# Second feed-forward layer, tokens 512 to 4607: GEMM2 as seven products behind all of GEMM1, w_out factors streamed from DRAM, output transposed

## The chip, the cores and the metric

One Trainium2 chip, one core. The metric is the device time of one execution in microseconds (us). Clock figures are the granted clock of TensorE as a share of full speed.

## The reference, cut to what matters

```python
attn_out = _attn_ref(q, k, v)                     # chunks of 64, 8 heads x 64
x = attn_out.transpose(0, 2, 1, 3).reshape(B * S, H * D)      # 4608 x 512, float32
...
h = x @ w_in          # layer 0: 512 -> 2048
x = (h * np.cos(h)) @ w_out                       # 2048 -> 512
...
h = x @ w_in          # layer 1, other weights
g = h * (1.0 / (1.0 + np.exp(-1.702 * h)))
return (g @ w_out).astype(np.float32)             # 4608 x 512
```

`GEMM1` is `x @ w_in` and `GEMM2` is `g @ w_out`. The change concerns GEMM2 of layer 1.

## The kernel before, in words

Every operand of a matmul is kept as a pair of a high part and a low part (`split`, lines 187 to 189: ScalarE copies the high part, VectorE subtracts it to get the low part), and every product of two pairs takes three matmuls: high by high, high by low, low by high. All large matmuls have a 128x128 stationary tile and 512 moving columns and add up in one PSUM bank.

The 4608 tokens are nine slices `j` of 512, the 2048 hidden columns are 16 tiles `f` of 128. In each layer the first slices run the ordinary way (`plain`): for each `f`, `gemm1` (12 matmuls, line 489), the activation, and two steps later `gemm2` (12 matmuls, line 587). The remaining slices run in pairs of 1024 tokens (`by_1024`, `pair_of_slices`). There GEMM1 of two slices and two hidden tiles is done with seven products instead of eight (the Strassen-Winograd scheme): sums and differences of the blocks of `x` (`right_factor`) and of `w_in` (`left_factors`, kept in DRAM as `wc`) are multiplied by six matmuls per product (`product`, line 837), and the results are added up in PSUM (`pu`, `pc`, `pb`) and on VectorE (`plus`, line 858).

GEMM2 is ordinary everywhere: 12 matmuls per `f` and slice. In a pair of slices, GEMM2 of slice `ja` stands between the products of GEMM1, one hidden pair behind (`run(6)`, `run(10)`, `run(8)` take its matmuls from a list), while the activations of slice `jb` are parked in SBUF (`park`); after the last pair of tiles comes GEMM2 of slice `jb` alone (`split_park`, `gemm2`). In layer 1 the activation is the stationary operand and `w_out` the moving one, so that the output has tokens on partitions and is stored by rows.

In layer 1, slice 0 is ordinary, and slices 1 to 8 are four pairs; I call each pair a stretch. During slice 0 `w_out` of layer 1 is still being converted from 64-bit floats (`split_w`: four VectorE operations, two or three of ScalarE, and one accumulating transfer from POOL's queue per tile), and the seven sums of `x` for the first stretch are made.

The order of the instructions on TensorE is the program's own (`manual_schedule` on PE). The other engines and the DMA queue of SyncE (SP, which issues nearly all transfers, in order) are ordered by a scheduler that places each instruction where it expects it to be ready. Buffers: eight temporaries of 128x512 (`tp`), two PSUM banks each for `pu` and for `pb`/`pc`, four for GEMM2's sums, three pairs for split activations (`gp`), and two buffers each of `xh` and `xl` (8 KB per partition) in `xp`, into which the factors of `w_in` are loaded one hidden pair ahead (`load_factors`).

## Time and profile before

| | |
|---|---|
| median of 3 runs | 1615.75 us (1613.85 to 1616.1) |
| the profiled execution | 1616.11 us, its span 1614.3 us |
| TensorE (PE) matmuls | 1574.7 us busy, 98% of the span |
| TensorE weight loads (PEld) | 1294.2 us, 80% |
| VectorE (DVE) | 989.0 us, 61% |
| ScalarE (ACT) | 885.1 us, 55% |
| POOL | 42.2 us, 3% |
| data moved | 322.14 MB, mean 200 GB/s |
| granted clock, mean | 0.992 |

The span is the time from the first to the last instruction of the profiled execution; its own time is 1.8 us longer. Matmuls are pipelined, so that the busy time of PE is longer than what PE needs: a matmul of 512 columns is shown with 389 ns, and the next one starts before it ends. The time per matmul is better read from the chain of waits, which gives whole runs of matmuls with their count.

### The profile page before, as it was taken

What the parts mean: (1) busy time and instruction counts of PE and PEld (TensorE: products, weight loads), DVE (VectorE), ACT (ScalarE), POOL (GpSimd) and SP (SyncE); (2) the same over time, 40 slices, a digit from 0 to 9 for tenths busy, and PEclk for the clock granted to TensorE, in tenths of its full rate; (3) what the DMA queues carried; (4) which work ended last, traced back from release to release, by engine and by line L of the source; (5) the groups of instructions that cost most, each with busy time, mean ns of one, the idle gap of its engine ahead of it and who ended that gap; (6) DMA issues with size and microseconds to landing.
All of it is one profiled execution on the core that took longest, in us unless ns stands there. A gap on an engine that the chain in (4) does not pass through costs nothing.

```text
span 1614.3 us, 23505 instructions
## 1 busy us (share of the span) xinstructions
PE 1574.7 (98%) x9024; PEld 1294.2 (80%) x9024; DVE 989.0 (61%) x1621; ACT 885.1 (55%) x1545; POOL 42.2 (3%) x53
## 2 busy tenths in 40 slices
PE   5898999999999999999999999999999999999998
PEld 4677888888888888888878888888888888888887
DVE  7796656787877687778665744455444544454442
ACT  6787656777765777567764633343334333433332
POOL 1221000000000000000000100000000000000000
PEclk9899999999999999999999999999999999999999
DMA  9999224468987798858899425440534053404210
GB/s 355 339 302 320 99 76 160 131 209 301 306 318 276 255 311 279 325 195 308 323 325 346 95 70 204 157 156 1 209 151 163 0 208 134 180 0 183 114 69 26
DMA packets 99328, 322.14 MB, mean 200 GB/s; under 512 B 10768, under 2 KB 10768, under 8 KB 84880
## 3 DMA queue, kind: packets, MB, share of 16 engines
q1 hardware_dynamic: 92448, 308.32, 52.9%
q0 software_dynamic: 6768, 12.32, 4.3%
q8 instruction: 71, 1.16, 0.3%
q14 instruction: 41, 0.34, 0.1%
HBM read 247.46 MB, written 60.82 MB: 191 GB/s over the span
## 4 chain that ended last, share of the span: by engine, by line
PE 92%; DMA 2%; issue 2%; ACT 2%; DVE 1%; SPq 0%; POOL 0%; POOLq 0%; DVEq 0%; ACTq 0%
PE y L587 47%; PE pu L837 19%; PE pc L837 9%; PE h L489 9%; PE pb L837 5%; PE x L411 1%; PE pt_ps L385 1%; PE s L304 1%; DMA i<-wt 1%; DMA raw_o<-w_out 1%; DMA wo<-wo 1%; ACT a L352 0%; DVE wt L234 0%; ACT a L340 0%; DVE wt L228 0%
## 5 line engine op out<-in xcount | busy, mean ns | idle before, releaser
L587 PE MATMUL y<-o,gh 128*128 128x512 f32 x1152 | 299.4, 389 | 0.0
L587 PEld LDWEIGHTS y<-o,gh 128*128 128x128 f32 x1152 | 216.3, 188 | 44.8
L837 PE MATMUL pu<-x_t,w_xh 128*128 128x512 f32 x672 | 207.7, 390 | 0.0
L587 PE MATMUL y<-gh,wo 128*128 128x512 f32 x768 | 203.1, 393 | 1.2 <-DMA wo<-wo 1.2
L587 PEld LDWEIGHTS y<-gh,wo 128*128 128x128 f32 x768 | 142.3, 188 | 32.1 <-ACT gh L188 2.5
L587 PE MATMUL y<-o,gl 128*128 128x512 f32 x576 | 158.4, 389 | 0.0
L189 DVE TENSOR_TENSOR gl<-park,gh 128x512 fp32r<-128x512 f32 x112 | 77.2, 689 | 116.6 <-PE y L587 115.6
L837 PEld LDWEIGHTS pu<-x_t,w_xh 128*128 128x128 f32 x672 | 125.6, 188 | 27.8 <-DVE part L858 1.9
L489 PE MATMUL h<-xh,i 128*128 128x512 f32 x384 | 132.3, 407 | 15.1 <-DVE r L528 10.1
L188 ACT ACTIVATE gh<-park 128x512 fp32r<-128x512 f32 x112 | 70.5, 629 | 126.9 <-PE y L587 126.7
L837 PE MATMUL pu<-x_t,w_xl 128*128 128x512 f32 x336 | 130.9, 390 | 0.0
L587 PEld LDWEIGHTS y<-o,gl 128*128 128x128 f32 x576 | 108.2, 188 | 22.4
L813 ACT ACTIVATE r<-part 128x512 f32<-128x512 f32 x96 | 60.3, 628 | 94.2 <-DVE part L858 94.2
L188 ACT ACTIVATE gh<-r 128x512 fp32r<-128x512 f32 x112 | 70.8, 632 | 69.1 <-DVE r L814 51.0
L189 DVE TENSOR_TENSOR gl<-r,gh 128x512 fp32r<-128x512 f32 x112 | 77.4, 691 | 49.6 <-ACT gh L188 47.1
L858 DVE TENSOR_TENSOR part<-pu,part 128x512 f32<-128x512 f32 x112 | 77.1, 689 | 47.3 <-PE pu L837 43.7
L587 PE MATMUL y<-gl,wo 128*128 128x512 f32 x384 | 105.8, 390 | 0.0
L489 PEld LDWEIGHTS h<-xh,i 128*128 128x128 f32 x384 | 75.2, 196 | 33.8 <-DVE r L528 11.7
L587 PE MATMUL y<-gh,o 128*128 128x512 f32 x384 | 101.5, 403 | 0.0
L858 DVE TENSOR_TENSOR part<-pc,part 128x512 f32<-128x512 f32 x56 | 38.6, 690 | 82.6 <-PE pc L837 68.4
L587 PEld LDWEIGHTS y<-gl,wo 128*128 128x128 f32 x384 | 72.1, 188 | 15.8 <-DVE gl L189 0.8
L587 PEld LDWEIGHTS y<-gh,o 128*128 128x128 f32 x384 | 71.8, 192 | 15.3
(122 smaller groups left out, 2776.3 us busy)
## 6 DMA issues: line engine op xcount, KB each, us to landing
w_xh<-wc SPq DMA_DIRECT2D x56, 1024.0 KB, 5.8
w_xl<-wc SPq DMA_DIRECT2D x56, 1024.0 KB, 8.1
wo<-wo SPq DMA_DIRECT2D x96, 512.0 KB, 4.9
qk<-qk SPq DMA_DIRECT2D x36, 512.0 KB, 6.3
raw_i<-w_in SPq DMA_DIRECT2D x32, 512.0 KB, 7.5
raw_o<-w_out SPq DMA_DIRECT2D x32, 512.0 KB, 9.3
wc<-i SPq DMA_DIRECT2D x64, 256.0 KB, 6.1
wc<-s_part SPq DMA_DIRECT2D x64, 256.0 KB, 4.6
```

The source lines that it names most:

```text
L188: nc.scalar.activation(out=hi, in_=src, func=AF.Copy)
L189: nc.vector.tensor_tensor(out=lo, in0=src, in1=hi.bitcast(F32), op=ALU.subtract)
L304: nc.tensor.matmul(out=s[e][o0:o0 + CH, w, h, :], lhsT=t[p0:p0 + CH, 0, h, o0:o0 + CH], rhs=t[p0:p0 + CH, 1, h, o0:o0 + CH],)
L385: nc.tensor.transpose(pt_ps[:, b, :], a[:, e, w, h0:h0 + 2, :].rearrange("p g k -> p (g k)"), ident)
L411: nc.tensor.matmul(out=xs[i][o0:o0 + CH, b, w, c * CH:(c + 1) * CH], lhsT=t[p0:p0 + CH, c, b, e, :], rhs=pt[p0:p0 + CH, e * (HP // 2) + b, ...
L489: nc.tensor.matmul(out=h, lhsT=a[:, w0], rhs=b[:, k, :], start=(k == 0 and i == 0), stop=(k == KD - 1 and i == 2),)
L587: nc.tensor.matmul(out=ys[d0], lhsT=a, rhs=b, start=(f == 0 and i == 0), stop=(f == NF - 1 and i == 2),)
L813: nc.scalar.activation(out=r, in_=h, func=AF.Sigmoid, scale=1.702)
L837: nc.tensor.matmul(out=out, lhsT=x, rhs=y, start=(start and k == 0 and n == 0), stop=(stop and k == 1 and n == 2), skip_group_check=True,)
L858: nc.vector.tensor_tensor(out=t, in0=more, in1=t, op=ALU.add)
```

## The change: what it does

1. GEMM2 of each stretch is made of seven products too. Its blocks are 1024 hidden columns by 512 tokens (`b11`, `b21`, `t1`, `t2` and three sums of these) and quarters of `w_out` (`a11`, `a12`, four sums, `a22`). A product is eight items (one per hidden pair `i`), an item is six matmuls (two output tiles by three), so GEMM2 of a stretch is 56 items. The order of products is 0, 1, 3, 2, 4, 5, 6.
2. All of GEMM1 of a stretch comes first (products of hidden pairs `i` and `i+1` interleaved), with nothing of GEMM2 between. The activations stay in SBUF as `G[i]` (the tiles `o0` to `o15`, where `w_out` stood), already as the differences `t1` and `t2`. Splitting them into high and low parts (`factor`) runs seven items ahead of the item that uses it (`RING`).
3. The seven factors of `w_out` are made during slice 0 (`left_factors2`, `half_factors2`) and stored in DRAM as `wq`, 256 KB at a time. In each stretch 16 chunks of `wc` and 14 chunks of `wq`, 1 MB each, are streamed through the four buffers of `xp` (`stream1`, `streamed`): a chunk is asked for when the one four before it has been used.
4. `w_out` is now the stationary operand in layer 1 too, and the output has its 512 columns on partitions; it is declared 512x4608, stored as blocks of 128x512 (`store_out`), and turned round on the host, outside the measured time.

Cut to its core (`right_factor` and `split` are unchanged):

```diff
-                ps_y.tile([P, N if layer == 0 else DM], F32, tag=f"y{d}", name=f"y{d}")
+                ps_y.tile([P, N], F32, tag=f"y{d}", name=f"y{d}") for d in range(nd)
...
-            if layer == 0:
-                a, b = ((wh[:, d], gh), (wl[:, d], gh), (wh[:, d], gl))[i]
-            else:
-                a, b = ((gh[:, d], wh), (gh[:, d], wl), (gl[:, d], wh))[i]
+            a, b = ((wh[:, d], gh), (wl[:, d], gh), (wh[:, d], gl))[i]
...
+    ORDER2 = (0, 1, 3, 2, 4, 5, 6)
...
+    def left_factors2(i):
...
+        def whole(k):
+            hi, lo = W[1, "o", 2 * i + k]
+            c[k] = tp.tile([P, DM], F32, tag="t", name="w32")
+            nc.vector.tensor_tensor(out=c[k], in0=hi.bitcast(F32), in1=lo.bitcast(F32), op=add)
...
+                nc.vector.tensor_tensor(out=o, in0=p, in1=q, op=op)
...
+            both = ap.tile([P, 2, DM], F32R, tag="a", name="s_part")
+            split(both[:, 0], both[:, 1], c["uw"[k]])
...
+            nc.sync.dma_start(
+                out=wq[m][i // 4][:, i % 4].bitcast(F32),
+                in_=src[:, :, half * H2:(half + 1) * H2].bitcast(F32),
+            )
...
+    def streamed(n, last):
+
+        ST.pop(n)
+        if n + 4 < NS or not last:
+            stream1((n + 4) % NS)
...
+        def factor(n):
...
+            if m < 4:
+                src = (b11, b21, t1, t2)[m]
+            else:
+                src = tp.tile([P, N], F32, tag="t", name="gs")
...
+                nc.vector.tensor_tensor(out=src, in0=a, in1=b, op=op)
+            split(hi, lo, src)
...
+        product(0, 1)
+        product(0, 0)
+        for m in rest:
+            gemm2(*m)
...
+        for m in (2, 3, 5):
+            product(0, m)
...
+        for i in range(NP - 1):
+            for m in (1, 4, 0, 2, 6, 3, 5):
+                product(i if m in (4, 6) else i + 1, m)
+            factor(i)
+        product(NP - 1, 4)
+        item(0)
+        factor(RING)
+        product(NP - 1, 6)
...
+        for n in range(1, len(items)):
+            item(n)
+            factor(n + RING)
+            if n % 7 in (1, 4) and n > 3 and todo:
+                right_factor(1, ja + 2, *todo.pop(0))
...
+    for i in range(NP):
+        at((1, 0, min(2 * i + 2, NF - 1)), half_factors2, i, 0)
```

Up to the third step of slice 0 of layer 1, all five engines have the same instructions in the same order as before. Three places after that:

TensorE, in the second stretch before: GEMM2 of slice `ja` (`y`, two moving parts of `w_out` per stationary tile `gh`) stands between the products `pc`, `pu`.

```order
L837 MATMUL pc_10980<-x_b221_10641,w_xh_10851 128x512
L837 MATMUL pc_10980<-x_b220_10640,w_xl_10853 128x512
L587 MATMUL y3_10858<-o2_8691,gh_10913 128x512 x2
L587 MATMUL y0_10855<-o2_8691,gl_10914 128x512
L587 MATMUL y1_10856<-o2_8691,gl_10914 128x512
```

TensorE at the same kind of place in the change, at the end of GEMM1 of the first stretch (`pu` of the last hidden pair, product 4), and on into GEMM2 (`q`, with the streamed factor `w_q`):

```order
L913 MATMUL pu<-x_t_9500,w_s 128x512
L978 MATMUL q_10411<-gh,w_q 128x512
L978 MATMUL q_10411<-gl,w_q 128x512
...
L913 MATMUL pu<-x_t_9704,w_s 128x512
...
L978 MATMUL q_10411<-gf,w_q 128x512 x3
L978 MATMUL q_10412<-gf,w_q 128x512 x3
```

Product follows product in GEMM1, one product of GEMM1 is left between the first two items, and from there items follow without a break.

VectorE in slice 0 of layer 1, between the activation of step 4 (`r<-h`) and that of step 5, before:

```order
L537 TENSOR_TENSOR r_9043<-h_9026,r_9043 128x512
L217 TENSOR_SCALAR wt_9049<-wt_9049 128x512
L222 TENSOR_SCALAR wt_9049<-wt_9049 128x512
L228 SCALAR_TENSOR_TENSOR wt_9049<-raw_o8_8796,wt_9049 128x512
L544 TENSOR_TENSOR gl_9087<-r_9043,gh_9086 128x512
L234 SCALAR_TENSOR_TENSOR wt_9049<-raw_o8_8796,wt_9049 128x512
L189 TENSOR_TENSOR x_t11_9191<-chain_9192,x_t10_9190 128x512
L189 TENSOR_TENSOR x_t11_9191<-chain_9196,x_t10_9190 128x512
```

and in the change:

```order
L236 SCALAR_TENSOR_TENSOR wt_9034<-raw_o7_8787,wt_9034 128x512
L801 TENSOR_TENSOR w32_9083<-o2_8705 128x512
L801 TENSOR_TENSOR w32_9085<-o3_8760 128x512
L548 TENSOR_TENSOR gl_9140<-r_9073,gh_9139 128x512
L814 TENSOR_TENSOR su_9087<-w32_9083,w32_9085 128x256
...
L814 TENSOR_TENSOR sw_9088<-w32_9085,su_9087 128x256
...
L191 TENSOR_TENSOR s_part_9093<-su_9087,s_part_9093 128x512
L230 SCALAR_TENSOR_TENSOR wt_9102<-raw_o8_8810,wt_9102 128x512
L191 TENSOR_TENSOR s_part_9096<-sw_9088,s_part_9096 128x512
```

Eight operations for the factors of `w_out` (two `w32`, four of 256 columns, two low parts `s_part`) now stand in every second step beside the conversion `wt`.

SP's queue at the beginning of the first stretch in the change: chunks of `w_in` factors (`w_s`) behind the last stores of `w_out` factors (`wq`) and slice 0's output:

```order
L857 DMA w_s_9753<-wc1_1_103 128x2x1024
L822 DMA wq2_1_131<-s_part_9729 128x2x256
L620 DMA out_0<-yo_9801 128x512
...
L620 DMA out_0<-yo_9810 128x512
L822 DMA wq3_1_133<-s_part_9729 128x2x256
L822 DMA wq4_1_135<-s_part_9732 128x2x256
L822 DMA wq5_1_137<-s_part_9732 128x2x256
L857 DMA w_s_9837<-wc1_2_104 128x2x1024
```

The chunk in the last row belongs to the third hidden pair; eight smaller transfers stand in front of it since the chunk before.

## Rows read from the trace of the kernel before

**Rows 1.** The page: its head, part 1, and part 4 by engine.

```profile
span 1614.3 us, 23505 instructions
...
PE 1574.7 (98%) x9024; PEld 1294.2 (80%) x9024; DVE 989.0 (61%) x1621; ACT 885.1 (55%) x1545; POOL 42.2 (3%) x53
...
PE 92%; DMA 2%; issue 2%; ACT 2%; DVE 1%; SPq 0%; POOL 0%; POOLq 0%; DVEq 0%; ACTq 0%
```

**Rows 2.** Stages: stretch, length, busy PE PEld DVE ACT POOL, clock, DMA share, GB/s.

```profile
966.84:1128.60 161.76, 161.76 (x715) 134.00 (x715) 75.51 (x114) 62.46 (x105) 0.00 (x0) 1.00 0.35 130
...
1452.00:1609.00 157.00, 157.00 (x694) 130.10 (x693) 60.55 (x89) 52.89 (x88) 0.00 (x0) 1.00 0.25 94
```

**Rows 3.** Chain of waits, second stretch: start, length, engine, tile, line, matmuls.

```profile
1234.76 43.52 PE y L587 x192
1278.28 1.36 PE pb L837 x6
```

**Rows 4.** Chain of waits, slice 0 of layer 1.

```profile
864.84 2.72 PE h L489 x12
867.56 2.72 PE y L587 x12
870.28 2.72 PE h L489 x12
...
946.44 2.72 PE h L489 x12
949.16 2.72 PE y L587 x12
951.88 1.36 PE pb L837 x6
```

**Rows 5.** VectorE in order of time, slice 0: start, length, line, operation.

```profile
897.05 0.69 DVE L774 TENSOR_TENSOR chain<-x,chain 128x512 f32<-128x512 f32 x1
897.65 0.42 DVE L222 TENSOR_SCALAR wt<-wt 128x512 uint32<-128x512 uint32 x1
897.99 0.68 DVE L544 TENSOR_TENSOR gl<-r,gh 128x512 fp32r<-128x512 f32 x1
898.59 0.68 DVE L228 SCALAR_TENSOR_TENSOR wt<-raw_o,wt 128x512 uint32<-128x512 uint32 x1
899.19 0.68 DVE L774 TENSOR_TENSOR chain<-x,chain 128x512 f32<-128x512 f32 x1
899.79 0.68 DVE L234 SCALAR_TENSOR_TENSOR wt<-raw_o,wt 128x512 uint32<-128x512 uint32 x1
```

**Rows 6.** VectorE operations on 256 columns: shortest, median, longest in ns.

```profile
L670 DVE TENSOR_TENSOR su<-w x8: 424/426/427, 164.2 to 335.8; 128x256 f32<-128x256 f32 x8
```

**Rows 7.** Stages of 40 us in slice 0, columns as in Rows 2.

```profile
880.00:920.00 40.00, 40.00 (x179) 33.12 (x178) 33.59 (x61) 25.39 (x46) 6.95 (x8) 1.00 0.57 150
920.00:960.00 40.00, 40.00 (x178) 33.16 (x177) 17.25 (x28) 16.14 (x28) 2.61 (x3) 1.00 0.25 73
```

**Rows 8.** Transfers of 1 MB in the first stretch, median us to landing.

```profile
w_xh<-wc SPq DMA_DIRECT2D x8, 1024.0 KB, 4.8
w_xl<-wc SPq DMA_DIRECT2D x8, 1024.0 KB, 6.8
```

**Rows 9.** The same for w_xl in the whole span.

```profile
L749 SPq DMA_DIRECT2D w_xl<-wc x56: 320/384/1628, 239.3 to 1531.5; - x56
...
DMA to landing us min/median/max: 4.8/8.1/13.3
```

**Rows 10.** Stores of left factors (s_part) to DRAM, 256 KB each.

```profile
L674 SPq DMA_DIRECT2D wc<-s_part x64: 319/320/1596, 166.0 to 782.5; - x64
...
DMA to landing us min/median/max: 2.0/4.6/6.6
```

**Rows 11.** ScalarE in order of time, slice 0.

```profile
911.61 0.62 ACT L243 ACTIVATE o<-wt 128x512 fp32r<-128x512 f32 x1
912.13 0.66 ACT L214 ACTIVATE wt<-raw_o 128x512 f32<-128x512 f32 x1
912.68 0.63 ACT L254 ACTIVATE o<-o 128x512 fp32r<-128x512 f32 x1
```

**Rows 12.** The end of the span, in order of time.

```profile
1609.73 0.39 PE L587 MATMUL y<-o,gl 128*128 128x512 f32 x1
1610.15 0.69 DVE L611 TENSOR_SCALAR yo<-y 128x512 f32<-128x512 f32 x1 [0.67 <-PE y L587]
```

More of the change, by code (lines that the diff above doesn't have):

```diff
@@ L128, in tile_chunk_attention_two_moe @@
     NU = qk.shape[0]
-    NT, DM = out.shape
+    DM, NT = out.shape
     NF = w1_in.shape[0]
@@ L182, in tile_chunk_attention_two_moe @@
     wo = [dr.tile([P, 2 * DM], F32R, name=f"wo_{f}") for f in range(NF)]
+    wq = [[dr.tile([P, 4, 2, 2 * P], F32R, name=f"wq{m}_{h}") for h in range(2)] for m in range(7)]
     J0 = 3
@@ L242, in p5 @@
             c["hi"], c["lo"] = w[:, :DM], w[:, DM:]
+            if layer == 1 and which == "o":
+                O1[f] = w
             nc.scalar.activation(out=c["hi"], in_=c["t"], func=AF.Copy)
@@ L567, in gemm2_list @@
         wh, wl = W[layer, "o", f]
-        nd = KD if layer == 0 else UB
+        nd = KD
         if f == 0:
             Y[layer, j] = [
-                ps_y.tile([P, N if layer == 0 else DM], F32, tag=f"y{d}", name=f"y{d}")
-                for d in range(nd)
+                ps_y.tile([P, N], F32, tag=f"y{d}", name=f"y{d}") for d in range(nd)
             ]
@@ L607, in flush_y @@
         for d, y in enumerate(ys):
-            o = tp.tile([P, N if layer == 0 else DM], F32, tag="t", name="yo")
+            o = tp.tile([P, N], F32, tag="t", name="yo")
             scale = -2.0 if layer == 0 else 1.0
@@ L616, in flush_y, with store_out @@
             else:
[L617 to L618 removed]
+                store_out(j, d, o)
+    def store_out(j, d, o):
+        nc.sync.dma_start(out=out[d * P:(d + 1) * P, j * N:(j + 1) * N], in_=o)
     steps = [(l, j, f) for l in range(2) for j in range(NB) for f in range(NF)]
@@ new lines, in half_factors2, with stream1 @@
+    def half_factors2(i, k):
+        if k == 0:
+            SF[i] = left_factors2(i)
+        for fn in SF[i][:-1] if k == 0 else SF.pop(i)[-1:]:
+            fn()
+    ST = {}
+    def stream1(n):
+        if n < 2 * NP:
+            t = xp.tile([P, 2, 4, 2 * P], F32R, tag=("xh", "xl")[n % 2], name="w_s")
+            src = wc[1][n // 2][:, :, 4 * (n % 2):4 * (n % 2) + 4, :]
+            nc.sync.dma_start(
+                out=t.bitcast(F32), in_=src.rearrange("t p o c -> p t o c").bitcast(F32)
+            )
+        else:
+            m, h = divmod(n - 2 * NP, 2)
+            t = xp.tile([P, 4, 2, 2 * P], F32R, tag=("xh", "xl")[n % 2], name="w_q")
+            nc.sync.dma_start(out=t.bitcast(F32), in_=wq[ORDER2[m]][h].bitcast(F32))
+        ST[n] = t
@@ L782, in tile_chunk_attention_two_moe @@
     PARK = {}
     def park(layer, i):
-        if layer == 0:
-            t = wp.tile([P, 2, N], F32, tag=f"o{4 + i}", name="park")
-        elif i < 2:
-            t = qkp.tile([P, 2, N], F32, tag="qk", name="park")
-        elif i < 4:
-            t = ap.tile([P, 2, N], F32, tag="a", name="park")
-        elif i < 6:
-            t = wp.tile([P, 2, N], F32, tag=f"i{NF - 6 + i}", name="park")
-        else:
-            return [vp.tile([P, N], F32, tag="v", name="park") for _ in range(2)]
+        t = wp.tile([P, 2, N], F32, tag=f"o{4 + i}", name="park")
@@ L1199, in tile_chunk_attention_two_moe @@
         rest = [(1, 0, NF - 2), (1, 0, NF - 1)]
+        stream1(2)
+        stream1(3)
         for ja in range(1, NB, 2):
-            last = ja + 2 == NB
-            step_extra = {}
-            if not last:
-                step_extra[0] = [(load_x1, (ja + 2,)), (load_x1, (ja + 3,))]
-                for n, (m, k) in enumerate(RIGHT):
-                    step_extra.setdefault(4 + n // 2, []).append((right_factor, (1, ja + 2, m, k)))
-            rest = by_1024(1, ja, rest, {}, step_extra, last)
-        for m in rest:
-            gemm2(*m)
-        flush_y(1, NB - 1)
-_OUTS = [((4608, 512), "float32")]
+            rest = stretch1(ja, rest, ja + 2 == NB)
+_OUTS = [((512, 4608), "float32")]
 def kernel(q, k, v, moe_w_in, moe_w_out, moe2_w_in, moe2_w_out):
```

162 lines of the change are left out of this document (157 added, 5 removed).

## The prediction, made before the change was run

> **What bounds the kernel now.** I read the page first, then the chain of waits, then the stages. In the head of the page PE is 98% busy and the other compute engines 55 to 61%; the chain that ended last lies on PE for 92% of the span [rows 1]. That alone doesn't say whether matmuls or gaps set the pace, so I looked at the stretches that the change touches: in each of them PE is busy all the time at a granted clock of 1.00 [rows 2]. The chain there is an unbroken run of matmuls: 192 of GEMM2 in 43.52 us, that is 226.7 ns each, and 1.36 us for the six of one product of GEMM1, the same rate [rows 3]. Slice 0 before it is just as dense: gemm1 and gemm2 in turn at 2.72 us per 12 [rows 4]. So in layer 1 time is the number of matmuls times 226.7 ns, as long as everything else keeps out of the way. VectorE and ScalarE have room in a stretch (75.5 and 62.5 us busy of 161.8) and so have the DMA engines (share 0.35) [rows 2]. Slice 0 is the fuller place: VectorE is busy 33.59 of 40 us in its first part and 17.25 in the next [rows 7].
>
> **What the change removes.** GEMM2 of a stretch was 2 slices x 16 tiles x 12 = 384 matmuls; it becomes 56 items x 6 = 336. GEMM1 stays at 336. Four stretches save 4 x 48 = 192 matmuls (the program's count of large and small matmuls falls from 7872 to 7680, the same 192). They have the same shape and the same kinds of operands, so I price them at the rate of the chain: **192 x 226.7 ns = 43.5 us** [rows 3]. The removed ones lie on the path that sets the end. Swapping stationary and moving operand in slice 0's gemm2 leaves count and shape as they were: nothing.
> The Trainium skill ("TensorE: Matmul & The Clock Gate", section "Wait — 56ns, not 53.3ns?") gives 215.7 ns for the step from one 512-column matmul to the next at 2.4 GHz. By it the saving would be an estimated 41.4 us and the result 2.1 us higher. The row is of this kernel and this is its full clock too, so the sum keeps 226.7.
>
> **What the change adds, VectorE first.** Its price is not the busy time in the rows. An operation of 512 columns is shown with 0.68 to 0.69 us, but in a dense run the next one starts 0.60 us after it (897.99, 898.59, 899.19, 899.79), and a short one of 0.42 us takes 0.34 of the queue [rows 5]. Sums of 256 columns are shown with 0.42 us [rows 6]; I take 0.34 likewise. ScalarE's step is 0.52 to 0.55 us [rows 11].
>
> *Slice 0.* The factors of `w_out` cost, per hidden pair, four operations of 512 columns and four of 256: 4 x 0.60 + 4 x 0.34 = 3.8 us, eight times, one every two steps (10.9 us of PE, [rows 4]). In the first 40 us, 61 operations show 33.59 us, which is 33.59 - 61 x 0.09 = 28.1 us of queue [rows 7, 5]; four pairs add 15.0, together 43 in 40 us. VectorE falls about 3 us behind and catches up in the next 40 us (17.25 - 28 x 0.09 + 15.0 = 30). What waits for it is gemm1 two steps on, which needs the PSUM bank of `h` that the sigmoid product has read: 10.88 - 2.72 = 8.2 us after gemm1 has ended, less about 1.3 us for ScalarE and that product, so 6.9 us of slack. Hidden, with 4 us to spare. From below nothing can be gained here. From above: with the full 0.69 and 0.42 us per operation, 33.59 + 4 x 4.44 = 51.4 in 40 us, 11.4 behind, less 6.9: 4.5 us. I take 0, since the dense rows are of this very place.
> ScalarE adds two copies per hidden pair, 1.1 us per 10.9: hidden. They reuse the two `s_part` buffers, so they wait for the stores of the pair before, 10.9 us earlier. Those stores land in 4.6 us, 6.6 at most [rows 10]; the new ones have runs of 1 KB instead of 2, and even twice as long, 13.2, would hold ScalarE 2.3 us, less than the slack of 6.9. The 56 stores are 14.7 MB in some 86 us, beside 150 and 73 GB/s [rows 7]: 0.
>
> *GEMM1 alone.* A round (seven products, 42 matmuls, 9.5 us) gives VectorE three additions, four activation products, two differences and one low part: 10 x 0.60 = 6.0 us, 63%. ScalarE has eight operations, 4.3 us. With GEMM2 gone from between, a bank that is read must be free two products later (2.72 us); the reading addition takes 0.69. Cost 0 where at most two others stand before it in the queue. At the beginning of the last three stretches only one product (1.36 us) lies between; the rest of a GEMM2 in VectorE's queue could cost 0 to 0.7 us three times. I take 0.
>
> *GEMM2.* An item lasts 1.36 us. Products 0 to 3 need one low part per item, 0.60 us; products 4 to 6 two operations, 1.2 us, still under 1.36. The 22 operations of `right_factor` for the next stretch stand early in the order, between the end of GEMM1 and the 16th item, where there is room: 22 x 0.60 = 13.2 us beside 16 x 0.6 = 9.6 in some 24 us. The ring gives each split the time of six items, 8.2 us. In a whole stretch VectorE has some 180 operations, 108 us of 152: hidden.
>
> *The stream.* Each stretch reads 30 MB instead of 16, about 1 MB per 5.1 us, 206 GB/s. A chunk is asked for when the one four before is used up. In GEMM1 that leaves eight products until it is needed, 10.9 us; in GEMM2 12 items, 16.3 us. 1 MB lands in 4.8 us, and the second of two asked for together in 6.8 [rows 8]; over the whole span 8.1 at the median and 13.3 at worst [rows 9]. The tight place is the first stretch, where stores and outputs stand before a chunk on SP. Bounds 0 and 13.3 - 10.9 = 2.4 us; the rows of the stretch itself are the nearest, so I take 0.5.
>
> *The end* stays: the last bank's copy of 0.69 us follows the last matmul [rows 12], then a store of the same size.
>
> **The sum.** Against the profiled execution: 1616.1 - 43.5 + 0.5 = 1573.1. That execution is 0.4 us over the median of the runs (1615.75), so the median should be **1573 us**. With the unknown costs at their ends (0 to 4.5, 0 to 2.1, 0 to 2.4) this case runs from 1572 to 1581, and single runs differ by 1 us to either side.
>
> **The rivals.**
> *VectorE at its full price.* If an operation holds the queue for its whole 0.69 us, slice 0 loses 4.5 us and nothing else does: in the late products 2 x 0.69 = 1.38 us per item against 1.36 is covered by the ring. 1573 + 4.5 = 1577.5. Against it: the dense rows step by 0.60 [rows 5].
> The Trainium skill ("VectorE: DVE Perf Modes", section "The TRN2 errata — SBUF-src ops pay a fixed extra latency per instruction") speaks for this rival: it gives 691 ns for a float32 sum of two tensors at 512 columns and says the latency shows between instructions. The busy time in the rows agrees with the 691, the step in the dense run doesn't. 8%.
> *GEMM1 without its filling.* With GEMM2 between the products a late addition cost nothing. Now, if two or three more operations stand before it on VectorE, 4 x 0.60 + 0.69 = 3.1 us against 2.72, each round loses 0.4 us or somewhat more, in 32 rounds some 12: 1585. For it: all readers of PSUM share two in-order queues. Against: 63% load. 10%.
> *The stream becomes the bound (slower than before).* If 1 MB took on average L us from request to landing in the stretches, each of the 32 rounds would wait L - 10.9. From L = 12.3 on this eats the whole 43.5 us; at 12.5 it gives 1624. For it: twice the data, and 13.3 us has been seen once under load [rows 9]. Against: 4.8 to 6.8 in a stretch, at a DMA share of 0.35 that would rise to about 0.6 [rows 2, 8]. 5%.
> *It doesn't save matmuls* is ruled out by the count.
>
> **How the numbers follow.** The forecast has 75%, VectorE's full price 8, GEMM1's gaps 10, the stream 5; 2 are left for stalls that cancel most of the gain. About 0.2% (3.2 us) is what a measurement of this kernel can tell from no change. All but the last two cases lie far below that: faster 0.94, same 0.01, slower 0.05. The range 1570.5 to 1584 holds the forecast with its bounds, the first rival and the mild half of the second.
>
> **What would show it.** Right: in the chain of the stretches, runs of PE without others, 152.3 us each (672 matmuls), VectorE 65 to 80% busy there, DMA share about 0.6, slice 0 still 86 us. Wrong in slice 0: waits of PE for the sigmoid product `r` or `gl`, and VectorE at 9 tenths over two slices of the page. Wrong in GEMM1: waits of `pu` or `pc` for `part`. Wrong in the stream: waits for DMA `w_s` or `w_q`, above all on the third hidden pair of the first stretch. The prediction as a whole is wrong if the matmuls in a stretch no longer follow each other at 226.7 ns.

## The result, and the profile after

The changed kernel takes **1574.51 us** (median of four runs, 1573.32 to 1575.34), the kernel before 1614.92 us (four runs, 1613.85 to 1616.1). The ratio is 0.9751, with a 95% interval of [0.9739, 0.9763]: faster by 40.4 us. The prediction was 1573.0 us with a range from 1570.5 to 1584. The profiled execution of the changed kernel took 1574.87 us, its span is 1573.1 us.

The head of the page and its lists by engine (busy time; the chain that ended last), after:

```profile
span 1573.1 us, 23852 instructions
...
PE 1531.2 (97%) x8832; PEld 1256.3 (80%) x8832; DVE 1169.5 (74%) x1953; ACT 958.3 (61%) x1669; POOL 42.3 (3%) x53
...
PE 85%; DVE 5%; DMA 5%; issue 3%; ACT 2%; SPq 0%; POOL 0%; POOLq 0%; DVEq 0%; ACTq 0%
```

They answer to [rows 1]. PE is as full as before (97% against 98%), and VectorE has risen from 61 to 74%. The chain is new in one way: a part of it now lies on VectorE and on DMA. The stages tell where. In the windows after (PE, PEld, DVE, ACT, POOL busy; granted clock, DMA share, GB/s) the first two rows are slice 0 of layer 1, the next three are the first three of the four stretches:

```profile
880.00:920.00 40.00, 39.77 (x176) 32.58 (x175) 36.28 (x72) 25.02 (x44) 6.00 (x7) 1.00 1.06 318
920.00:960.00 40.00, 39.27 (x172) 31.63 (x171) 39.85 (x78) 24.12 (x42) 3.70 (x5) 1.00 0.91 258
966.84:1119.20 152.36, 151.54 (x669) 125.07 (x668) 113.88 (x181) 78.21 (x133) 0.00 (x0) 1.00 0.73 249
1119.20:1271.50 152.30, 152.30 (x674) 126.02 (x673) 114.25 (x182) 78.92 (x133) 0.00 (x0) 1.00 0.66 232
1271.50:1423.80 152.30, 152.30 (x673) 126.04 (x672) 112.12 (x178) 78.91 (x133) 0.00 (x0) 1.00 0.63 221
```

The stretches are what they should be: 152.30 us for 672 matmuls, VectorE 74 to 75% busy, DMA share 0.63 to 0.73; before they took 161.8 us [rows 2]. PE is busy all the time from the second stretch on; in the first it has gaps of 0.82 us together. Slice 0 is not as it was [rows 7]: the DMA share went from 0.57 to 1.06 and from 0.25 to 0.91, VectorE has next to no idle time left in the second row (0.15 us), and PE has gaps (39.77 and 39.27 of 40). The chain inside the stretches is an unbroken run of matmuls of GEMM2, 74.80 us for 330, 226.7 ns each, as in [rows 3]:

```profile
1037.22 74.80 PE q L978 x330
1189.58 74.80 PE q L978 x330
1341.93 74.80 PE q L978 x330
```

What PE still waits for, from slice 0 to the end (weight load and what released it: us in total, times, longest):

```profile
PEld h L493 <- DVE r L541: 1.4, 3, 0.7
PEld pb L913 <- DMA w_s<-wc: 1.2, 1, 1.2
PEld y L587 <- DVE gl L548: 1.2, 1, 1.2
PEld pu L913 <- DVE part L886: 0.5, 3, 0.2
```

A weight load may wait while PE still has work, so these times are upper bounds of what PE lost; they are the list of places. The first and third rows lie in slice 0 or at its end (`r`, three times; `gl` of its last tile), the second is the chunk of the third hidden pair in the first stretch. The last row is one wait of 0.2 us at the end of GEMM1 in each of the first three stretches; the kernel with 4 stores (below) has the same three and loses nothing, so they cost PE nothing. No stretch after the first has a wait of PE for the stream.

**A better yardstick than the span.** Layer 0 and all that comes ahead of slice 0 is the same work in every kernel here, but it doesn't end at the same moment in each execution. In time order of PE, the first matmul of slice 0 starts before and after at

```profile
864.68 0.39 PE L489 MATMUL h<-xh,w 128*128 128x512 f32 x1
```

```profile
863.82 0.39 PE L493 MATMUL h<-xh,w 128*128 128x512 f32 x1
```

So I count from there to the end of the span: 1614.3 - 864.68 = 749.6 us before, 709.3 after. The predicted 43.5 us would leave 749.6 - 43.5 = **706.1**; the changed kernel loses 3.2 us against that. The experiments below are read by this count, which takes out the early part's variation of some 2 us (4 with the kernel whose stores POOL issues).

Each row of the table below is one execution. Three kernels in it have the same slice 0 and the same stores as the changed kernel, which loses 3.2 us: they lose 3.1 us (GEMM1's products twice), 4.0 us (lead of three chunks) and 752.1 - 43.5 - 706.1 = 2.5 us (192 more matmuls). So rows that differ by 1 us or so can't be told apart.

### The profile page after: what moved, and what is told of

Read it like the earlier page. It is cut to its first block, busy times and chain, and to the rows that moved or that the text cites. A ratio compares the mean times of both kernels' runs of the same rounds, so it can differ in the third digit from the quotient of the medians.

```text
span 1573.1 us, 23852 instructions
## 1 busy us (share of the span) xinstructions
PE 1531.2 (97%) x8832; PEld 1256.3 (80%) x8832; DVE 1169.5 (74%) x1953; ACT 958.3 (61%) x1669; POOL 42.3 (3%) x53
## 4 chain that ended last, share of the span: by engine, by line
PE 85%; DVE 5%; DMA 5%; issue 3%; ACT 2%; SPq 0%; POOL 0%; POOLq 0%; DVEq 0%; ACTq 0%
PE y L587 23%; PE q L978 19%; PE pu L913 11%; PE pu L1075 8%; PE h L493 7%; PE pc L913 5%; PE pc L1075 4%; PE pb L913 3%; PE pb L1075 2%; DMA raw_o<-w_out 1%; PE x L415 1%; DMA o<-wt 1%; PE s L308 1%; PE pt_ps L389 1%; DMA i<-wt 1%
## 5 line engine op out<-in xcount | busy, mean ns | idle before, releaser
L978 PE MATMUL q<-gf,w_q 128*128 128x512 f32 x768 | 179.3, 389 | 0.0
L978 PEld LDWEIGHTS q<-gf,w_q 128*128 128x128 f32 x768 | 144.2, 188 | 29.9
L913 PE MATMUL pu<-x_t,w_s 128*128 128x512 f32 x576 | 141.7, 389 | 0.0
L913 PEld LDWEIGHTS pu<-x_t,w_s 128*128 128x128 f32 x576 | 107.9, 188 | 22.8 <-DVE part L886 0.5
L978 PE MATMUL q<-gh,w_q 128*128 128x512 f32 x384 | 124.0, 389 | 0.0
L1075 PE MATMUL pu<-x_t,w_xh 128*128 128x512 f32 x288 | 89.6, 392 | 0.0
L978 PEld LDWEIGHTS q<-gh,w_q 128*128 128x128 f32 x384 | 72.1, 188 | 14.9
L895 DVE TENSOR_TENSOR g<-part,r 128x512 f32<-128x512 f32 x96 | 65.8, 685 | 21.6 <-ACT r L894 21.6
L493 PE MATMUL h<-xl,i 128*128 128x512 f32 x192 | 77.3, 403 | 0.3 <-DVE xl L436 0.3
L978 PE MATMUL q<-gl,w_q 128*128 128x512 f32 x192 | 74.7, 389 | 0.0
L587 PE MATMUL y<-gl,o 128*128 128x512 f32 x256 | 70.5, 390 | 0.7 <-DVE gl L548 0.7
```

What stands on the lines that cost most here:

```text
L493: nc.tensor.matmul(out=h, lhsT=a[:, w0], rhs=b[:, k, :], start=(k == 0 and i == 0), stop=(k == KD - 1 and i == 2),)
L587: nc.tensor.matmul(out=ys[d0], lhsT=a, rhs=b, start=(f == 0 and i == 0), stop=(f == NF - 1 and i == 2),)
L895: nc.vector.tensor_tensor(out=dest, in0=h, in1=r, op=ALU.mult)
L913: nc.tensor.matmul(out=o, lhsT=x, rhs=y, start=(m < 3 and k == 0 and n == 0), stop=(m in (1, 5, 6) and k == 1 and n == 2), skip_group_chec ...
L978: nc.tensor.matmul(out=o, lhsT=x, rhs=y, start=(m < 3 and i == 0 and k == 0), stop=(m in (1, 5, 6) and i == NP - 1 and k == 2), skip_group ...
L1075: nc.tensor.matmul(out=out, lhsT=x, rhs=y, start=(start and k == 0 and n == 0), stop=(stop and k == 1 and n == 2), skip_group_check=True,)
```

## The experiments

What each kernel's profile gives by this count:

| kernel | first matmul of slice 0 | span | from there to the end | over 706.1 | median, us |
|---|---|---|---|---|---|
| changed kernel | 863.82 | 1573.1 | 709.3 | 3.2 | 1574.51 |
| 192 more matmuls | 863.14 | 1615.2 | 752.1 | 46.0 | 1617.11 |
| no work for the factors, all stores | 863.90 | 1575.3 | 711.4 | 5.3 | 1576.14 |
| all the work, 4 of 56 stores | 862.48 | 1568.5 | 706.0 | -0.1 | 1571.44 |
| all stores at half the bytes | 863.91 | 1572.1 | 708.2 | 2.1 | 1574.31 |
| stores issued by POOL | 866.58 | 1593.8 | 727.2 | 21.1 | 1596.15 |
| two pairs later | 863.10 | 1572.9 | 709.8 | 3.7 | 1574.94 |
| three pairs later | 864.95 | 1573.1 | 708.2 | 2.1 | 1573.10 |
| three pairs later, spread | 862.74 | 1574.3 | 711.6 | 5.5 | 1574.11 |
| two later, the rest shifted | 863.26 | 1572.0 | 708.7 | 2.6 | 1573.82 |
| GEMM1's products twice | 862.80 | 1572.0 | 709.2 | 3.1 | 1573.70 |
| GEMM1's products three times | 863.59 | 1620.5 | 756.9 | 50.8 | 1621.88 |
| lead of three chunks | 862.69 | 1572.8 | 710.1 | 4.0 | 1574.71 |

My theory after the two traces was: PE's pace sets the stretches; slice 0 lost its 2 us to VectorE's in-order queue, and the stores on SP cost only the late chunk. The rival: the stores cost all of it.

### Do matmuls alone set the pace of a stretch?

```diff
-                for k, (x, y) in enumerate(((ah, hi), (ah, lo), (al, hi))):
+                for k, (x, y) in enumerate(((ah, hi), (ah, lo), (al, hi)) * (2 if m == 0 else 1)):
```

> The 48 matmuls of the first product of GEMM2 are issued twice in each of the four stretches, 192 more in all, and accumulate twice, so the second layer's output is another one. Theory (PE alone sets the pace at 226.7 ns per matmul): 192 x 226.7 ns = 43.5 us more, about 1618. Rival (the stream or VectorE sets the pace of GEMM2): part of the 43.5 us is absorbed, time well below 1618.

Measured: 1617.11 us, a ratio to the kernel before of 1.0014 [1.0003, 1.0024]; against the changed kernel 42.6 us more in the medians and 752.1 - 709.3 = 42.8 by the count from slice 0. In its chain GEMM2 runs like this:

```profile
1037.27 84.32 PE q L978 x372
```

84.32 / 372 = 226.7 ns. Theory holds: what the change took away can be put back at the same price, and nothing absorbs it. The 0.7 us that are missing to 43.5 lie in slice 0 and at the late chunk, where this execution waited less (weight loads 1.2, 1.1 and 0.9 us in all for `r`, `gl` and `w_s`, against 1.4, 1.2 and 1.2). That this kernel is back at the time of the one before is the saving seen from the other side.

### VectorE or the stores?

Two kernels, each with one of the two suspects left out. First the stores without the work, raw parts of `w_out` in place of the factors:

```diff
...
         return [
-            lambda: whole(0), lambda: whole(1), lambda: sums(0), lambda: sums(1),
-            lambda: parts(0), lambda: parts(1), stores,
-        ]
+        return [stores]
```

> Left out: the VectorE and ScalarE work for the factors of w_out in slice 0; the same 56 stores carry raw parts of w_out instead, so the second layer's output is another one. Theory (VectorE's in-order queue is what slice 0 lost its 2 us to): the three waits of PE for r in slice 0 (1.4 us) and the wait for the gl of its last tile (1.2 us) vanish, VectorE between 920 and 960 us falls from 39.85 to about 22 us busy, and the time is about 2 us under the changed kernel, some 1572.5. The wait for the third hidden pair's chunk in the first stretch (1.2 us) stays, since the stores on SP are as many as before. Rival (the stores and their bytes hold slice 0, not VectorE): waits and time as in the changed kernel, 1574.5.

Measured: 1576.14 us, 0.9763 [0.975, 0.9777], not faster than the changed kernel, and 5.3 us over the full saving by the count. **Both the theory and the rival missed.** The three waits for `r` and the wait for the chunk went, but one wait grew to more than all of them. In time order of VectorE and of PE around the end of slice 0 (idle time ahead and its releaser in brackets):

```profile
952.30 0.69 DVE L776 TENSOR_TENSOR chain<-x,x 128x512 f32<-128x512 f32 x1 [12.84 <-DMA x<-y]
```

```profile
953.65 1.63 PE L587 MATMUL y<-gl,o 128*128 128x512 f32 x4 [3.45 <-DVE gl L548]
```

The first row says that VectorE had nothing to do for 12.84 us: the operation at the head of its queue needed a tile of `x`. The second says that PE waited 3.45 us for VectorE all the same. In the chain of waits that load stands behind the stores:

```profile
915.49 12.49 DMA wq<-o
...
928.00 8.79 DMA wq<-o
...
945.36 6.92 DMA x<-y
...
952.91 0.69 DVE gl L548
```

These stores needed no sums, so nothing spread them out any more; they stand ahead of the load on SP, and by the chain SP came to the next of them when earlier ones had landed, after 12.49 and 8.79 us (the stores before took 2.0 to 6.6 [rows 10]). Behind the wait of PE there is a second loss, of the clock:

```profile
940.00:950.00 10.00, 10.00 (x45) 8.10 (x44) 0.00 (x0) 0.60 (x1) 0.00 (x0) 1.00 1.02 310
950.00:960.00 10.00, 6.55 (x22) 5.07 (x22) 6.29 (x10) 2.23 (x4) 0.00 (x0) 0.83 0.82 296
```

The granted clock fell from 1.00 to a mean of 0.83 in the window of the wait, and its 22 matmuls kept PE busy for 6.55 us instead of 22 x 0.2267 = 5.0. Wait and clock together are 5.0 of the 5.3 us.

Then the stores left out, with all the work of VectorE and ScalarE:

```diff
-                store(m, src, half)
+                if m == 0 and i < 4:
+                    store(m, src, half)
...
-            nc.sync.dma_start(out=t.bitcast(F32), in_=wq[ORDER2[m]][h].bitcast(F32))
+            nc.sync.dma_start(out=t.bitcast(F32), in_=wq[0][0].bitcast(F32))
```

> Left out: 52 of the 56 stores of the factors of w_out; every load of factors reads the one piece that is stored, so the second layer's output is another one. VectorE's and ScalarE's work is as in the changed kernel. Theory (VectorE's queue cost slice 0 its 2 us, the stores on SP only the chunk's lateness): the waits of PE for r and gl stay (about 2 us together), the wait for the third pair's chunk (1.2 us) goes, time about 1573.4. Rival (copies that wait for stores still under way hold ScalarE, behind it VectorE, and so slice 0): the waits for r and gl go too, time about 1571.5.

Measured: 1571.44 us, 0.9732 [0.9719, 0.9745]; its four runs (1570.36 to 1571.7) all lie under the changed kernel's four (1573.32 to 1575.34). By the count 706.0 us: **nothing is left of the loss.** Both slice 0's waits and the late chunk are gone, as the rival had it. The rival's path is not seen, though: in the changed kernel ScalarE's copies of `s_part` in slice 0 wait for VectorE's sums (`su`, 7.0 us in 7 waits) and never for a store. The windows of slice 0:

```profile
880.00:920.00 40.00, 40.00 (x178) 33.14 (x177) 37.32 (x76) 25.32 (x45) 5.27 (x6) 1.00 0.65 179
920.00:960.00 40.00, 40.00 (x177) 32.90 (x177) 40.00 (x78) 24.28 (x43) 3.56 (x4) 1.00 0.43 125
```

VectorE is busy 40.00 of 40 us, more than in the changed kernel, and PE has no gap at all. A full queue is not a late queue. So VectorE's work for the factors costs nothing by itself, as predicted, and my theory after the traces was wrong: I had taken the busiest engine for the cause.

How the stores reach PE can be followed in the changed kernel. The low part of a `w_out` tile goes through a DMA that POOL issues (`o<-wt`, 12 between 865 and 951 us). From issue to landing (least, median, most) it took, in the changed kernel and with 4 stores:

```profile
DMA to landing us min/median/max: 3.5/6.2/8.3
```

```profile
DMA to landing us min/median/max: 3.3/3.6/8.1
```

The tile that it reads (`wt`) is one of the eight temporaries (`tp`), and so is the tile of ScalarE's sigmoid copy `r`: by the code, `r` can be written only when the transfer that last used its buffer is done. `r` waited for that twice in the changed kernel, 2.5 us in all, and once, 1.1 us, with 4 stores; behind it in ScalarE's queue stands the copy of `s_part`, and for that VectorE waits:

```profile
899.29 0.69 DVE L191 TENSOR_TENSOR s_part<-sw,s_part 128x512 fp32r<-128x512 f32 x1 [1.02 <-ACT s_part L190]
911.22 0.69 DVE L191 TENSOR_TENSOR s_part<-sw,s_part 128x512 fp32r<-128x512 f32 x1 [0.65 <-ACT s_part L190]
```

With 4 stores the first hole is 0.68 us and the second isn't there: 1.0 us less. VectorE has no idle time after that in which to make it good, so the same 1 us shows up at PE, in the waits for `r` and, at the end of slice 0, for `gl`.

Counted from the first matmul of slice 0, VectorE comes to the low part of the last tile at 94.14 us in the changed kernel and at 92.23 with 4 stores, 1.9 us apart, which is what PE lost in slice 0. The two holes are 1.0 of this. Another 0.5 us comes from a load of `x`, which landed at 6.23 us in the one execution and at 5.74 in the other, and for which VectorE waited; it was issued before the first store in both kernels, and that the stores delayed it isn't shown. The rest stays open.

The stores alone don't make these waits either. In the kernel with all stores and no work the low parts landed later still, after 7.5 us at the median, and neither ScalarE's `r` nor PE waited for them. What slice 0 lost takes both, the late transfers and the work that keeps VectorE full and uses the same eight temporaries; whether the full VectorE or the shared temporaries count more wasn't tried apart.

### Bytes or number?

```diff
-                out=wq[m][i // 4][:, i % 4].bitcast(F32),
-                in_=src[:, :, half * H2:(half + 1) * H2].bitcast(F32),
+                out=wq[m][i // 4][:, i % 4, :1].bitcast(F32),
+                in_=src[:, :1, half * H2:(half + 1) * H2].bitcast(F32),
...
```

> Left out: the low parts of the factors of w_out are not stored, and the loads take the high parts twice, so the second layer's output is another one. All 56 stores are there, each with half the bytes (128 KB), in runs of 1 KB as before, and all work of VectorE and ScalarE. Theory A (bytes: the DMA engines are full in slice 0): the waits for r, gl and the chunk go or nearly, 706 to 707 us from the first matmul of slice 0 to the end, time about 1571.5 to 1572.5. Theory B (the number of stores that SP has to issue in order, 0.5 us and more each): the waits stay, 709 us, about 1574.5.

Measured: 1574.31 us, 0.9744 [0.973, 0.9757]; 708.2 by the count, between the two theories. The wait for the chunk is gone, the waits in slice 0 are not:

```profile
PEld h L493 <- DVE r L541: 1.6, 3, 0.9
PEld y L587 <- DVE gl L548: 0.9, 1, 0.9
```

They stay although the DMA share of the two windows fell to 0.87 and 0.62. The two low parts that hold `r` are as late as before: issued at 890.5 and 902.4 us, they landed after 7.6 and 7.9 us, against 7.5 and 7.7 in the changed kernel and 7.2 and 3.3 with 4 stores. The chunk was asked for 101.7 us after the first matmul of slice 0 instead of 104.5. So in this execution half the bytes take away the late chunk (1.1 us of the 3.2) and not the 2 us of slice 0; these are there with 56 stores of either size and gone with 4. In the medians (1574.31 and 1574.51) nothing is gained. How the 56 stores make the low parts late stays open.

### Another queue for the stores

```diff
-            nc.sync.dma_start(
+            nc.gpsimd.dma_start(
                 out=wq[m][i // 4][:, i % 4].bitcast(F32),
```

> Nothing is left out: the 56 stores of the factors of w_out are issued by POOL instead of SP, same bytes in the same order. After the runs before this one slice 0 and the chunk behind it are held by the stores, not by VectorE's work (without 52 of the stores the profile had no wait left there). Theory A (order on SP: loads and chunks stand behind stores that SP can't issue yet): with the stores on POOL's own queue the waits for r, gl and the chunk go, and from the start of slice 0 to the end of the span it takes some 706 to 707 us instead of 709.3, a time about 1572. Theory B (DMA engines full: 318 GB/s at a share of 1.06 between 880 and 920 us, against 150 GB/s and 0.57 before): the same bytes take the same time whoever issues them, the waits stay and 709 us remain, about 1574.5; POOL's own loads of o stand behind the stores and could add to it.

Measured: 1596.15 us, 0.9886 [0.9869, 0.9902]: 21.6 us slower than the changed kernel. Neither theory foresaw that; I had named POOL's loads of `o` as something that "could add to it", and they are a large part of it. POOL's queue around 895 us:

```profile
894.43 1.46 POOL L822 DMA_DIRECT2D wq<-o  x2 [8.22 <-DMA o<-wt]
895.86 2.85 POOL L822 DMA_DIRECT2D wq<-s_part  x4
898.70 0.95 POOL L261 DMA_DIRECT2D o<-wt  x1
```

A store of a finished tile waits until the tile's own low part has landed (38.9 us in 11 waits over slice 0), and the next tile's low part stands behind it; ScalarE's `r` waited for low parts four times, 7.5 us in all. ScalarE's copies of `s_part` waited for the stores themselves three times, 12.5 us in all; the longest of these waits, 8.8 us, stands in the chain before PE's longest one:

```profile
962.74 9.31 DMA wq<-s_part
```

PE then waited 13.4 us in five places, up to 5.59 us at once. Most of the rest is clock. In three windows around those waits:

```profile
905.00:912.00 7.00, 5.00 (x15) 3.94 (x16) 6.95 (x13) 4.16 (x9) 4.16 (x6) 0.76 0.58 157
944.00:955.00 11.00, 9.41 (x34) 7.63 (x35) 11.00 (x22) 6.36 (x12) 5.55 (x8) 0.84 0.90 249
975.00:985.00 10.00, 7.87 (x22) 5.75 (x23) 8.93 (x18) 4.67 (x9) 3.18 (x5) 0.59 0.73 236
```

the mean granted clock is 0.76, 0.84 and 0.59, that is the lower level for a part of each. Their 15, 34 and 22 matmuls kept PE busy for 5.00, 9.41 and 7.87 us instead of 3.40, 7.71 and 4.99 at 226.7 ns each: 6.2 us of clock beside 13.4 us of waits, 19.6 of the 21.1 us together. The run doesn't tell SP's order from the bytes, since it made a worse order of its own.

### Moving the work for the factors

Four versions make some of the pairs later, all with the full computation. Two pairs in the first four rounds of GEMM1:

```diff
+            if rest and i < 4:
+                half_factors2(NP - 2 + i // 2, i % 2)
             factor(i)
...
```

> Nothing is left out: the factors of the last two hidden pairs (6 and 7) are made in the first four rounds of GEMM1 of the first stretch instead of at the end of slice 0. Theory: the end of slice 0 has VectorE free again, so the wait for gl of its last tile (0.9 us of the end) and the late chunk (1.1 us) go, while the first four rounds of GEMM1 bear 1.9 us more of VectorE each (6.0 + 1.9 = 7.9 of 9.5 us): about 1572.5, 1 to 2 us under the changed kernel. Rival (GEMM1 has no room for late additions): waits for part in these four rounds, 0.4 us or more each, and a time equal to the changed kernel's 1574.5 or over it.

Measured: 1574.94 us, 0.9755 [0.9741, 0.9768]; 709.8. The rival's result: the chunk was in time, but PE waited 1.5 us for `part` in the first rounds.

Three pairs there, the others every three steps:

```diff
+            if rest and 0 < i < 4:
+                half_factors2(NP - 4 + i, 1)
+            if rest and i < 3:
+                half_factors2(NP - 3 + i, 0)
             factor(i)
...
```

> Nothing is left out: the factors of the last three hidden pairs are made in the first four rounds of GEMM1 of the first stretch, and those of the other five are spread over slice 0, one every three steps instead of two. Theory: slice 0 loses nothing (VectorE there 33.6 - 5.5 + 3.8 x 40/16.3 = some 37 shown of 40 us at most, with dense queue 0.60 per operation), the late chunk goes, and the rounds of GEMM1 that hold the second half of one pair and the first of the next bear up to 6.0 + 3.8 = 9.8 of 9.5 us: 0.3 us each for two or three rounds, so about 1572, 2 to 3 us under the changed kernel. Rival (GEMM1 has no room): over 1574.5, with waits for part in rounds 1 to 3 of the first stretch.

Measured: 1573.10 us, 0.9745 [0.9732, 0.9758]; 708.2, PE waits 0.8 us for `part`. About half of the 2 to 3 us that were expected; its interval overlaps the changed kernel's, so no gain is shown.

Half a pair per round, in six rounds:

```diff
+            if rest and i < 6:
+                p = NP - 3 + i // 2
+                if i % 2 == 0:
+                    SF[p] = left_factors2(p)
+                for fn in SF[p][:4] if i % 2 == 0 else SF.pop(p)[4:]:
+                    fn()
             factor(i)
...
```

> Nothing is left out: the factors of hidden pairs 0 to 4 are made one pair every three steps of slice 0, those of pairs 5 to 7 in the first six rounds of GEMM1 of the first stretch, half a pair in each. In the version with three pairs in rounds 0 to 3 a round bore all 3.8 us of a pair and lost about 0.8 us in a wait for part. Theory: with 2.6 us of extra VectorE in rounds 0, 2, 4 and 1.2 us in rounds 1, 3, 5 (8.6 and 7.2 of 9.5 us) these waits go, slice 0 loses at most 0.3 us, and from the start of slice 0 to the end it takes 706 to 707 us instead of 709.3: about 1572, 2 to 3 us under the changed kernel. Rival (in the first stretch any addition to VectorE or SP costs, since SP issues outputs, stores and chunks there): waits for part or w_s of 1 to 2 us, time 1573 to 1574.5.

Measured: 1574.11 us, 0.9749 [0.9734, 0.9763]; 711.6, a miss. PE now waited 1.9 us for `gf` in GEMM2, which neither theory named: from round 3 on `s_part` and the first `gf` tiles take turns in the same two buffers, so copies of the later pairs came in between (this is read from the code and the name of the waiting tile; it wasn't tried apart). Slice 0, where only five pairs were left, still lost 1 us or so.

Six pairs in slice 0, each two steps later, and two in rounds 0 to 2 in small steps:

```diff
-    for i in range(NP):
-        at((1, 0, min(2 * i + 2, NF - 1)), half_factors2, i, 0)
+    for i in range(NP - 2):
+        at((1, 0, 2 * i + 4), half_factors2, i, 0)
...
+                if more and (7 * i + n) % 3 < 2:
+                    more.pop(0)()
```

> Nothing is left out. In slice 0 six of the eight pairs of factors are made, each two steps later than in the changed kernel, so that the first stores stand on SP behind the loads of w_out and x that they held up; the last two pairs are made in rounds 0 to 2 of GEMM1 of the first stretch, one short step behind two of three products (2.5 us of VectorE more in a round, 8.5 of 9.5 us). Theory (slice 0 loses time because stores stand on SP and on the DMA engines ahead of loads in its first half, where the DMA share was 0.57 before and 1.06 after): from the first matmul of slice 0 to the end of the span 706 to 707.5 us instead of 709.3, time 1571.5 to 1573. Rival (the stores cost the same wherever they stand, as long as there are 56): 709 us or more, time 1574 to 1575.

Measured: 1573.82 us, 0.9743 [0.973, 0.9757]; 708.7. By the count it lies between the two, too near to both to tell, and its waits are the old ones at other places (0.5 us for `r`, 1.2 for `part`). None of the four beats the changed kernel by more than these runs can tell; what is left to be gained is 3 us at most, and moving the work mostly moved the wait.

### How much VectorE work does GEMM1 carry?

```diff
-            nc.vector.tensor_tensor(out=dest, in0=h, in1=r, op=ALU.mult)
+            for _ in range(2):
+                nc.vector.tensor_tensor(out=dest, in0=h, in1=r, op=ALU.mult)
```

> Nothing is left out: in GEMM1 of layer 1 each of the four products of h with its sigmoid is done twice, so that a round of seven products holds 14 operations of VectorE instead of 10. This tests the second rival of the prediction, that GEMM1 without GEMM2 between loses time to late additions. By the step of 0.60 us a round has 8.4 us of VectorE in 9.5 and loses nothing (time within 2 us of 1574.5); at 0.69 us each it would have 9.7, lose 0.2 us in each of 32 rounds, and give about 1580; and if lateness in the in-order queue counts and not the load, 0.4 us and more per round, 1587 or over.

Measured: 1573.70 us, 0.9744 [0.9724, 0.9763], and 709.2 by the count, the same as the changed kernel. PE waited once for `part` (0.9 us, for ScalarE), at the beginning of the first stretch, and then no longer for the late chunk; in the rounds it had no wait, so 14 operations in a round cost nothing there. All waits of PE from slice 0 on:

```profile
PE pc L914 <- ACT part L882: 0.9, 1, 0.9
PE y L587 <- DVE gl L548: 0.5, 1, 0.5
PE h L493 <- DVE r L541: 0.3, 1, 0.3
```

With three times each:

> Nothing is left out: in GEMM1 of layer 1 each of the four products of h with its sigmoid is done three times, so that a round of seven products (9.52 us of PE) holds 18 operations of VectorE instead of 10, more than fit. The loss then measures what one operation of 512 columns holds of the queue: at the step of 0.60 us a round takes 10.8 us, 1.28 us over, in some 31 rounds 40 us, about 1614; at the shown 0.69 us (the prediction's first rival) 12.4 us, 2.9 us over, 90 us, about 1664; where PE is not held by VectorE at all, 1574.5.

Measured: 1621.88 us, 1.005 [1.003, 1.0069], 47.4 us more than the changed kernel, where the step of 0.60 us gave 40 and the full 0.69 gave 90. PE waits where the prediction's rival on GEMM1 said it would:

```profile
PE pu L914 <- DVE part L886: 21.1, 18, 2.2
PE pu L914 <- DVE g L896: 13.0, 12, 1.4
```

In a stretch of GEMM1 where VectorE is the one that sets the pace, it did 82 operations in 50 us:

```profile
1145.00:1195.00 50.00, 44.25 (x189) 35.00 (x190) 49.15 (x82) 19.79 (x35) 0.00 (x0) 1.00 0.50 182
```

50 / 82 = 0.61 us each. That is the dense step of [rows 5] (0.60) and not the 0.69 us of busy time. The edge lies between 14 and 18 operations in a round of 9.52 us; the change's 10 are well inside.

### The lead of the stream

```diff
-        if n + 4 < NS or not last:
-            stream1((n + 4) % NS)
+        if n + 3 < NS or not last:
+            stream1((n + 3) % NS)
```

> Nothing is left out: a chunk of the stream is asked for when the one three before it is used up, instead of four. In GEMM1 the lead of every second chunk falls from 10.9 to 2.7 us, of the others to some 6.8 to 8.2, in GEMM2 from 16.3 to 10.9. This measures how long a chunk takes in a stretch, on which the third rival stands (the stream becomes the bound from L = 12.3 us). With L of 4.8 to 6.8 us some 28 to 32 chunks wait L - 2.7 = 2.1 to 4.1 us: 60 to 130 us more, 1635 to 1705, and waits for w_s of that length. If a chunk took 10.9 us or more, as the rival needs, the waits would be 8 us and the time over 1800. In GEMM2 no waits by theory, waits of 1.4 us and more by the rival.

Measured: 1574.71 us, 0.9748 [0.973, 0.9765]; no difference. The edit didn't do what I wanted. In SP's time order two chunks in GEMM1 of the second stretch are asked for in the changed kernel and here at

```profile
1125.66 0.38 SPq L857 DMA_DIRECT2D w_s<-wc  x1
1127.02 0.36 SPq L857 DMA_DIRECT2D w_s<-wc  x1
```

```profile
1125.30 0.38 SPq L857 DMA_DIRECT2D w_s<-wc  x1
1126.66 0.36 SPq L857 DMA_DIRECT2D w_s<-wc  x1
```

which is the same moment in the stretch: this execution's slice 0 began 1.13 us earlier and lost some 0.8 us more up to there. In both kernels SP issues each of the two 0.02 us after the matmul of `pu` that it waited for has ended, and there are two buffers for each of the two kinds of chunk in both. So here it is the release of a buffer that sets the lead, and the place of the call in the program doesn't change it. So the experiment says nothing on a shorter lead; for the third rival the trace has to do (below).

## Why the prediction was right, and by how much not

**The matmuls (43.5 us): right.** Stretches of 152.30 us, 226.7 ns per matmul in their chains, and 42.8 us for 192 put back. The Trainium skill's 215.7 ns ("TensorE: Matmul & The Clock Gate", section "Wait — 56ns, not 53.3ns?") would have priced them at an estimated 41.4 us; the chain of the kernel with 192 more shows 226.7 again.

**VectorE in slice 0 (0, bounds 0 to 4.5): right in its 0, wrong in the room that is left.** With 4 stores the whole work was there and nothing was lost. The prediction had VectorE 3 us behind, a slack of 6.9 and "4 us to spare". Where PE first waited for `r`, VectorE came to it 42.27 us after the first matmul of slice 0 before the change, at 46.93 with 4 stores and at 48.61 in the changed kernel, and PE lost 0.5 us there: 4.7 us behind without a wait, 6.3 with one, a slack of some 5.8 us and 1.1 to spare. VectorE is dense from 920 us to the end of the slice, so the lateness of anything ahead of it in its queue goes through to PE. The sign that the prediction named for an error of this term came: waits for `r` and `gl`, and VectorE at 8, 9 and 8 tenths in three slices of the page. It did not tell VectorE's work from what makes it late.

**The stores in slice 0 (0): wrong, the one term of the wrong kind.** "The 56 stores are 14.7 MB in some 86 us, beside 150 and 73 GB/s [rows 7]: 0." With them the changed kernel loses 3.2 us, late chunk included, and with 52 of them left out nothing; some 0.5 us of this may be the execution's and not theirs (above). The bytes were reckoned rightly (318 and 258 GB/s were reached), but what counted was what got late while they were under way: the chunk behind them in SP's order, and the low parts of `w_out`, which took 6.2 us instead of 3.6. How the stores delay the low parts, which POOL issues, is not shown. I had looked at the stores as a load on the DMA engines and at their landing as a wait for `s_part`, and not at the other transfers that they make late.

**The stream (0.5, bounds 0 to 2.4): right place, half of what was measured.** One wait, at the third hidden pair's chunk of the first stretch, as named; 1.1 us. SP issued that chunk at 968.33 us behind four outputs and the last stores:

```profile
961.36 5.30 SPq L620 DMA_DIRECT2D out<-yo  x4
966.71 1.52 SPq L822 DMA_DIRECT2D wq<-s_part  x3
968.33 0.59 SPq L857 DMA_DIRECT2D w_s<-wc  x1
```

**The sum.** Predicted for the profiled execution: 1573.1 us; measured 1574.87. The losses are 3.2 us instead of 0.5, and slice 0 began 0.86 us earlier than before, which no step of the change did: 1573.1 + 2.7 - 0.9 = 1574.9. That a third of the missed loss is made good by the earlier start is luck.

**The rivals.** VectorE at its full price is ruled out: 0.61 us per operation in a saturated queue. The rule of the Trainium skill that spoke for it ("VectorE: DVE Perf Modes", section "The TRN2 errata — SBUF-src ops pay a fixed extra latency per instruction") agrees with the 0.68 to 0.69 us of busy time in the rows and not with the rate at which operations follow each other here. GEMM1 without its filling did not come; the run with 14 operations per round shows that there is room for a load spread evenly, and the one with 18 that PE waits for `part` when the round is overfull. What the rival meant, a late addition in a round that is not full, came where factors were put into the rounds in blocks: PE waited 1.5 us for `part` at a reckoned 7.9 of 9.5 us (two pairs later). The stream as the bound did not come either: between 960 and 1420 us the 48 chunks of GEMM1 landed in 4.8 us at the least, 5.9 at the median and 9.8 at most, where it needed 12.3 on average:

```profile
DMA to landing us min/median/max: 4.8/5.9/9.8
```

## What to carry to other kernels

Price a new transfer not only by its bytes and by who waits for it, but by every load that stands behind it in the issuing engine's order, and by the transfers in flight beside it; leave those out in one run and the work in another before blaming the busiest engine. An engine at 40.00 of 40 us can cost nothing, and one that idles 12.84 us can be the one that PE waits for. And where differences of 1 to 3 us are in question, count from the point where the kernels begin to differ: here the part ahead of it varied by as much.

## What the runs showed of the hardware that I had not expected

- VectorE's operations of 512 float32 columns are shown with 0.68 to 0.69 us, but a saturated queue does 82 in 50 us, 0.61 each.
- What a wait of PE costs is not only its length. In slice 0 of the changed kernel, with single gaps of 0.23 and 0.73 us, the granted clock stayed at 1.00. Behind the gaps of 3.45 us in one experiment, and of 2.09, 2.10 and 5.59 us in another, it fell to the lower level for a time, and this added 1.6 us to the first and 6.2 to the 13.4 us of the second; a gap of 1.46 us between these left it at 1.00. The length of the gap alone doesn't decide. With GEMM1's products three times PE has eight gaps of 2.12 or 2.19 us, and the clock fell behind two of them; around a gap of 2.12 us at 1007.94 us and one of 2.19 us at 1042.96 us the windows are

```profile
1004.00:1014.00 10.00, 7.88 (x29) 6.07 (x28) 9.05 (x16) 3.38 (x7) 0.00 (x0) 0.83 0.51 158
1040.00:1050.00 10.00, 7.57 (x32) 5.59 (x31) 9.49 (x16) 6.39 (x13) 0.00 (x0) 1.00 0.57 210
```

- SP asked for a chunk at the same moment of the stretch whether the program placed the request three or four chunks ahead: 0.02 us after the matmul that it waited for.
